# A fused attention and MLP kernel on one core: batch 0 in 24 single-exp slots, row sums of batch 1 moved out of the head, four MLP chunks begun early, and a weight matrix loaded by column halves

## The chip, the cores and the metric

The kernel runs on one core of a Trainium2 chip. The metric is the device time of one execution in microseconds (us), median of several; lower is better. The profile is of one execution of its own, and its span is about 2 us shorter than the device time. PE is TensorE (PEld its weight loads), DVE is VectorE, ACT is ScalarE, POOL is GpSimd, SP is SyncE, which issues the loads of q, k, v, U and V. The "granted clock" is the share of full TensorE clock that the throttle allowed.

## The reference, cut to what matters

```python
# q, k, v: 8 batches, 12 heads, 448 rows, 64 columns
q_n, k_n = rmsnorm(q, g_q), rmsnorm(k, g_k)
attn = softmax(q_n @ k_n.T / 8);  x = attn @ v            # per head; then heads side by side: 448 x 768
u  = x + (x.T @ U @ V).T                                  # U: 448 x 32, V: 32 x 448
out = u + relu(u @ w_ch1) @ w_ch2                         # w_ch1: 768 x 3072, w_ch2: 3072 x 768
```

## The kernel before

Heads are handled in pairs, six pairs to a batch; two pairs make a tile `t` (four heads of q, k and v). For each pair: squares and row sums, `rsqrt` (Ln and Exp on ACT), scaling, transposes on PE, scores in four blocks of keys, one exp of 112 x 896 per block, then values. The MLP of batch b runs as a generator `mlp(b)` whose pieces are woven between the pieces of `attention(b + 1)`. Batch 0's attention has no MLP to be woven with: this is the head. Score blocks have two PSUM buffers, called score banks below.

```python
def mlp(b):
    for hc in range(KH):                                   # 24 chunks: one "unit" of six matmuls each
        ph = ps_mm.tile([P, n], FP32, tag="mm")
        ...                                                # six matmuls, then relu: even on ACT, odd on DVE
        yield n
    for i in range(3 + par):                               # second product: row tile by row tile
        for half in range(2): ...                          # 24 matmuls each, four units; add u; store

def head():
    load(0, 2); load(1); load_v(0); load(2); load_mix(); ...      # load_mix loads U and V
    heat(NWARM)                                            # 16 warming matmuls, results unused
    ...
    rsqrt(1)
    setup_v()                                              # ACT casts V to bf16: waits for V's load
    scale(1, 0)
    ...
    for p in range(2, 7):                                  # one pair after another
        scores(p, (0, 1)); expo(p, 0); mix_a(0, p - 2); transposes(p + 1); expo(p, 1)
        ...
        values(p - 1, 0); heat(NH); scores(p, (2, 3)); expo(p, 2); values(p - 1, 1); mix_b(0, p - 2)
        expo(p, 3); scale(t + 1, odd); squares(t + 2, ALL, (odd,)); reduce(t + 2, ALL, (odd,))
        if p < 6: heat(NH)
        ...
# main: head(); load_w2 (row chunks) 0 to 2; then
rest = [(1, lambda i=i: mix_u(0, i)) for i in range(4)] + attention(1, 1)      # pairs 7 to 11
weave(fill, total * FA0, rest)
```

`squares` (POOL from tile 2 on) and `reduce` (DVE) make the row sums; `scale` is DVE, a `tensor_tensor` with both inputs in SBUF. `mix_u` adds the mixing term to x: PE, then two additions on DVE.

## Time and profile before

| | before |
|---|---|
| median of the first runs | 626.93 us (625.84 to 628.16) |
| span of the profile | 625.2 us |
| batch 0's MLP begins / batch 1's MLP begins | 56.0 us / 126.5 us |
| PE not busy, 11 to 57 us | 10.4 of 46 us |
| PE not busy, 57 to 126 us | 3.8 of 69 us |
| PE not busy, 126 to 205.8 us | 0.5 of 79.8 us |

The page of the profile has the span in 40 equal slices of 15.6 us; each digit is a busy share in tenths, and in the PEclk row the granted clock.

```profile
span 625.2 us, 11231 instructions
...
PE   5698999999999999999999999999999999999996
...
DVE  4688778146455466735546375935646365442211
ACT  5575662045430565145530465225441265302100
...
PEclk9599999999999999999999999999999999999999
DMA  9999988215535355655345356545155311040011
```

From the fifth slice on (62.5 us) every digit of PE up to the last slice is 9, so nearly all of the slack is at the front. The second clock digit is 5: in the second slice PE ran at about half its clock. The windows view gives busy time by stretch (the columns are the stretch, its length, the busy times of the engines with instruction counts, granted clock, DMA share and GB/s):

```profile
11.00:57.00 46.00, 35.59 (x397) 20.22 (x398) 35.10 (x85) 30.89 (x47) 25.56 (x23) 0.78 1.16 237
57.00:126.00 69.00, 65.16 (x577) 38.45 (x577) 44.23 (x97) 24.60 (x37) 16.68 (x13) 1.00 0.75 159
126.00:205.80 79.80, 79.27 (x605) 42.47 (x603) 40.85 (x91) 28.85 (x42) 14.32 (x9) 1.00 0.41 94
```

From 126 us on PE is the limit. The chain that ended last (start, us, what), up to 70 us, shows one thing that holds the head: V's load. ACT's next exps stand behind V's cast.

```profile
9.29 13.00 DMA Vf<-in_moe_V_dram
22.32 0.99 ACT V_90 L116
23.30 1.62 ACT E_96 L235 x2
```

The clock, again by the windows view, in stretches that follow the trace's clock record:

```profile
9.81:13.23 3.42, 1.16 (x12) 0.59 (x12) 2.40 (x7) 1.50 (x4) 0.00 (x0) 0.99 1.12 223
13.23:16.64 3.41, 1.76 (x14) 0.78 (x12) 2.76 (x5) 3.41 (x5) 0.25 (x1) 0.50 1.14 232
...
33.71:37.12 3.41, 3.00 (x44) 1.87 (x43) 2.62 (x6) 3.02 (x5) 0.23 (x1) 1.00 1.17 246
```

The clock stood at 0.50 for 20.5 us, until 33.7 us. In the kernel before, the throttled times read within the kernel are multiples of 3.41 us (20.5 us), so stretches of that length, cut where the clock changes, are called windows from here on.

### The profile page before, as it was taken

Reading aid. Unit: us, or ns where it says so; the run is one execution under the profiler, and the core shown is the slowest. Engines: PE = TensorE matmul, PEld = TensorE weight load, DVE = VectorE, ACT = ScalarE, POOL = GpSimd, SP = SyncE. Lnnn points to the kernel's source line nnn. Section 1 sums busy time; section 2 is a strip of 40 time slices with the busy share of each in tenths; the row PEclk is TensorE's granted clock in tenths of the full one; section 3 lists DMA queues with packets and bytes.
Section 4 is the critical chain, followed back from the end, with each engine's and each line's share of the span. In section 5 each row is a group of like instructions: output and inputs, shape, how many; then the busy total and the mean of one; then the engine's idle time right before and its main releaser. Section 6 shows DMA issues by size and latency. Waiting matters only on the chain.

```text
span 625.2 us, 11231 instructions
## 1 busy us (share of the span) xinstructions
PE 595.9 (95%) x4751; PEld 330.6 (53%) x4751; DVE 333.4 (53%) x735; ACT 235.6 (38%) x352; POOL 121.4 (19%) x101
## 2 busy tenths in 40 slices
PE   5698999999999999999999999999999999999996
PEld 2344555644555565544465555554556556554563
DVE  4688778146455466735546375935646365442211
ACT  5575662045430565145530465225441265302100
POOL 2656143011211121202221033303131020000000
PEclk9599999999999999999999999999999999999999
DMA  9999988215535355655345356545155311040011
GB/s 193 234 246 225 195 185 172 77 40 118 104 80 139 56 118 119 164 81 104 85 75 160 62 118 115 129 116 111 28 125 140 92 32 30 26 102 0 1 51 50
DMA packets 97913, 67.20 MB, mean 107 GB/s; under 512 B 54104, under 2 KB 94280, under 8 KB 97864
## 3 DMA queue, kind: packets, MB, share of 16 engines
q1 hardware_dynamic: 89732, 57.06, 40.3%
q0 software_dynamic: 7872, 9.44, 8.7%
q8 instruction: 37, 0.61, 0.4%
q14 instruction: 12, 0.10, 0.0%
q10 hardware_dynamic: 260, 0.00, 0.0%
HBM read 52.19 MB, written 11.01 MB: 101 GB/s over the span
## 4 chain that ended last, share of the span: by engine, by line
PE 79%; DVE 7%; DMA 6%; ACT 4%; issue 2%; POOL 1%; SPq 0%; POOLq 0%
PE po L351 33%; PE ph L336 30%; PE o L254 7%; PE sc L230 6%; DMA qkT<-qkn 2%; DMA Vf<-in_moe_V_dram 2%; DMA qk<-in_q_dram 2%; DVE qkn L201 1%; DVE osb L355 1%; DVE rstd L187 1%; ACT E_95 L235 1%; PE pu L293 1%; ACT hT L339 1%; ACT E_96 L235 1%; PE pt L214 1%
## 5 line engine op out<-in xcount | busy, mean ns | idle before, releaser
L351 PE MATMUL po<-w2b,hT 128*128 128x384 bf16 x1344 | 234.2, 326 | 2.9 <-DVE osb L355 2.9
L351 PEld LDWEIGHTS <-hT 128*128 128x128 bf16 x1344 | 126.8, 98 | 91.9 <-issue 13.5
L336 PEld LDWEIGHTS <-w1b 128*128 128x128 bf16 x1152 | 105.8, 98 | 105.6 <-issue 16.6
L339 ACT ACTIVATE hT<-ph 128x384 bf16<-128x384 f32 (+1 forms) x96 | 52.3, 545 | 253.0 <-PE ph L336 253.0
L181 POOL TENSOR_TENSOR sq<-qk 112x1024 f32<-112x1024 f32 x40 | 75.7, 1893 | 363.2 <-DVE rstd L187 232.2
L235 ACT ACTIVATE E_96<-sc 112x896 bf16<-112x896 f32 x96 | 85.9, 914 | 51.4 <-PE sc L230 51.4
L341 DVE TENSOR_SCALAR hT<-ph 128x384 bf16<-128x384 f32 (+1 forms) x96 | 59.6, 623 | 81.1 <-PE ph L336 80.3
L235 ACT ACTIVATE E_95<-sc 112x896 bf16<-112x896 f32 x96 | 85.8, 913 | 32.8 <-PE sc L230 32.7
L230 PE MATMUL sc<-qkT 64*112 64x448 bf16 x384 | 63.9, 386 | 9.7 <-ACT E_96 L235 4.4
L201 DVE TENSOR_TENSOR qkn<-qk,rstd 112x512 bf16<-112x512 f32 x88 | 59.6, 717 | 7.1 <-ACT rstd L193 7.0
L187 DVE TENSOR_REDUCE rstd<-sq 112x16 f32<-112x1024 f32 x44 | 53.2, 1209 | 2.4 <-POOL sq L181 2.0
L230 PEld LDWEIGHTS <-qkT 64*112 64x112 bf16 x384 | 22.0, 127 | 48.1 <-issue 43.3
L257 DVE RECIPROCAL rec<-o 128x4 f32<-128x4 f32 x96 | 17.1, 178 | 42.8 <-PE o L254 42.4
L254 PEld LDWEIGHTS <-E_95 112*128 112x128 bf16 x768 | 30.8, 99 | 9.8 <-issue 3.3
L254 PEld LDWEIGHTS <-E_96 112*128 112x128 bf16 x768 | 30.4, 99 | 7.6 <-issue 1.3
L336 PE MATMUL ph<-u_1555,w1b 128*128 128x512 bf16 x144 | 33.4, 379 | 0.0
L336 PE MATMUL ph<-u_3351,w1b 128*128 128x512 bf16 x144 | 33.3, 379 | 0.1
L336 PE MATMUL ph<-u_5057,w1b 128*128 128x512 bf16 x144 | 33.3, 379 | 0.0
L336 PE MATMUL ph<-u_6723,w1b 128*128 128x512 bf16 x144 | 31.2, 379 | 0.0
L336 PE MATMUL ph<-u_359,w1b 128*128 128x384 bf16 x144 | 27.1, 325 | 2.6 <-DVE hT L341 1.9
L336 PE MATMUL ph<-u_4220,w1b 128*128 128x384 bf16 x144 | 25.8, 326 | 0.1
L336 PE MATMUL ph<-u_5926,w1b 128*128 128x384 bf16 x144 | 25.8, 326 | 0.0
(111 smaller groups left out, 402.2 us busy)
## 6 DMA issues: line engine op xcount, KB each, us to landing
vt<-in_v_dram SPq DMA_DIRECT2D x22, 448.0 KB, 6.8
qk<-in_q_dram SPq DMA_DIRECT2D x21, 448.0 KB, 4.5
qk<-in_k_dram SPq DMA_DIRECT2D x21, 448.0 KB, 6.0
w1b<-in_moe_w_ch_dram POOLq DMA_DIRECT2D x6, 768.0 KB, 18.3
w2b<-in_moe_w_ch_dram POOLq DMA_DIRECT2D x6, 768.0 KB, 10.2
out_dram<-osb SPq DMA_DIRECT2D x8, 336.0 KB, 2.8
out_dram<-osb SPq DMA_DIRECT2D x8, 288.0 KB, 2.6
out_dram<-osb SPq DMA_DIRECT2D x8, 240.0 KB, 2.6
```

The source lines that it names most:

```text
L181: nc.gpsimd.tensor_tensor(sqs[t, s][:, hs], qks[t][:, s, hs], qks[t][:, s, hs], OP.mult)
L187: nc.vector.tensor_reduce(rstds[t][:, s, hs].rearrange("p h j -> p (h j)"), sqs[t, s][:, hs].rearrange("p h (j d) -> p (h j) d", d=D), AX, ...
L201: nc.vector.tensor_tensor(qkns[t][:, pr, s].rearrange("p j h d -> p h j d"), qk[:, s, hp].rearrange("p h (j d) -> p h j d", d=D), rstd[:, ...
L214: nc.tensor.transpose(pt.rearrange("d s (j p) -> d (s j) p", j=NJ)[:, i, :], qkn[:, i, :], ident[:SP, :SP])
L230: nc.tensor.matmul(sc[:, hh, 0:S], kT[pp, kc * SP:(kc + 1) * SP], qT[pp, :], start=True, stop=True)
L235: nc.scalar.activation(Es[p % NE][:, :, PAD + kc * S:PAD + (kc + 1) * S], scs.pop((p, kc))[:, :, 0:S], AF.Exp, scale=float(D) ** 0.5)
L254: nc.tensor.matmul(o[:, i, :], E[:, hh, c:c + P], va[:, hl, kc, :], start=(kc == 0), stop=(kc == NJ - 1))
L257: nc.vector.reciprocal(rec, o[:, :, D])
L336: nc.tensor.matmul(ph, w1b[:, dc, hc * P:(hc + 1) * P], u[:, dc, :], start=(dc == 0), stop=(dc == KD - 1))
L339: nc.scalar.activation(hT[:, hc, 0:n], ph, AF.Relu)
L341: nc.vector.tensor_relu(hT[:, hc, 0:n], ph)
L351: nc.tensor.matmul(po, hT[:, hc, i * P:(i + 1) * P], w2b[:, hc, hs], start=(hc == 0), stop=(hc == KH - 1))
```

## The change

Its intent: run the head at ACT's pace, one exp per slot, with everything else fitted between; let values lag by two pairs; take V's cast off ACT's critical place; take tiles 3's and 4's row sums out of the head; use the score banks, free after the last exp, to begin the MLP; issue w2 later and by column halves, because its area now also holds squares.

```diff
-    early = w2b[:, 0:11, :]...                    # squares of tiles 0 and 1
+    early = w2b[:, 0:22, :]...                    # squares of tiles 0 to 3
-    NE, NV, NWARM, NH = 2, 3, 16, 3
-    FA, FM, NPE, FA0 = 0.77, 0.09, 14, 0.5
+    NE, NV, NWARM, NH = 3, 3, 16, 2
+    FA, FM, NPE, FA0 = 0.77, 0.09, 14, 0.66
...
-    def load_w2(i):           # four rows of 128
+    def load_w2(half, i):     # eight rows of 128, one half of the columns
...
+        order = [(i, h) for h in range(2) for i in range(n)] if b == 0 else [(i, h) for i in range(n) for h in range(2)]
...
 # attention(b), within a pair p of tile t:
+            if t + 1 < NT and not odd:
+                add(0, reduce, t + 1, ALL, (1,))
             add(1, expo, p, 1)
...
+            if t + 1 < NT and odd:
+                add(0, scale, t + 1, 1)
+                add(0, cast_v, t + 1)             # POOL cast, now right behind the scale
...
 # head:
+        at(1, squares, 1, ALL, (1,));  at(1, reduce, 1);  at(1, yield_port, 0, 1);  at(1, squares, 2)
+        at(2, heat, NH);  at(3, rsqrt, 1);  at(3, scale, 1, 0);  ...;  at(4, heat, NH)
+        at(5, transposes, 2);  ...;  at(10, values, 0, 0);  at(11, values, 0, 1);  at(11, setup_v)
+        ...;  at(21, values, 4, 0);  at(22, values, 4, 1);  ...
+        for n in range(24):
+            expo(*divmod(n, 4))
+            for piece in fill[n]: piece()
+            if n + 2 < 24: scores((n + 2) // 4, ((n + 2) % 4,))
+        first(0, range(0, 3), True)               # MLP chunks 0 to 3, in two score tiles
+        values(5, 0);  values(5, 1);  mix_b(0, 4);  first(0, (3,), False);  first(1, range(0, 4), True)
+        ...;  mix_b(0, 5);  reduce(3);  rsqrt(3)
+        first(0, (5,), False);  first(1, (5,), False)
+        scale(3, 0);  scale(3, 1);  squares(4, ALL, (0,))
...
+        late = {6 + i: [(load_w2, *divmod(i, 3))] + ([(mix_u, 0, i - 1)] if 0 < i < 5 else []) for i in range(6)}
+                rest = [(4, lambda: (transposes(6), reduce(4, ALL, (0,)), squares(4, ALL, (1,))))] + attention(1, late)
```

`yield_port` is a tiny POOL copy that reads a scaled tile, so that POOL's next work starts after DVE's scale. Each entry of `late` runs at the end of its pair. The diff holds more that the cut leaves out: four of six copies of `mix_b` went from ACT to DVE, relus 1, 3 and 5 of batch 0 from DVE to ACT, V's load went ahead of the first load of v, and w1 comes in four loads instead of six.

More of the change, by code (lines that the diff above doesn't have):

```diff
@@ L76 @@
     spare = hT.rearrange("p k n -> p (k n)").bitcast(FP32).rearrange("p (t s h e) -> p t s h e", t=2, s=3, h=HG)
-    early = w2b[:, 0:11, :].rearrange("p k n -> p (k n)")[:, 0:8192].bitcast(FP32).rearrange("p (t s h e) -> p t s h e", t=2, s=2, h=HG)
+    early = w2b[:, 0:22, :].rearrange("p k n -> p (k n)")[:, 0:16384].bitcast(FP32).rearrange("p (t s h e) -> p t s h e", t=4, s=2, h=HG)
     Ub = consts.tile([P, 2, 4, rank], BF16, name="Ub")
@@ L136, in load_w1 @@
     def load_w1(i):
-        c = slice(512 * i, 512 * (i + 1))
+        c = (slice(0, 512), slice(512, 1024), slice(1024, 2048), slice(2048, 3072))[i]
         nc.gpsimd.dma_start(w1b[:, :, c], w1r[:, :, c])
-    def load_w2(i):
-        c = slice(4 * i, 4 * (i + 1))
-        nc.gpsimd.dma_start(w2b[:, c, :], w2r[:, c, :])
+    def load_w2(half, i):
+        c, d = slice(8 * i, 8 * (i + 1)), slice(half * HALF, (half + 1) * HALF)
+        nc.gpsimd.dma_start(w2b[:, c, d], w2r[:, c, d])
     NT, NP = B * 3, B * 6
@@ L175, in squares @@
             if (t, s) not in sqs:
-                sqs[t, s] = early[0:SP, t, s] if t < 2 else norm.tile([SP, HG, NJ * D], FP32, tag="sq", name="sq", bufs=1)
+                sqs[t, s] = early[0:SP, t, s] if t < 4 else norm.tile([SP, HG, NJ * D], FP32, tag="sq", name="sq", bufs=1)
             if t < 2:
@@ L321, in mix_b @@
             nc.tensor.matmul(pu[:, i * P:(i + 1) * P], xt[i][:, cs], ident, start=False, stop=(i == 2))
-        nc.scalar.activation(us[b][:, dc, :], pu, AF.Copy)
+        if dc in (0, 5):
+            nc.scalar.activation(us[b][:, dc, :], pu, AF.Copy)
+        else:
+            nc.vector.tensor_copy(us[b][:, dc, :], pu)
     def store(b, c0, c1, osb, r0):
@@ L332, in mlp @@
         u, n = us[b], (384, 512)[par]
-        for hc in range(KH):
+        for hc in range(0 if b else 4, KH):
             ph = ps_mm.tile([P, n], FP32, tag="mm")
@@ L337, in mlp @@
                                  start=(dc == 0), stop=(dc == KD - 1))
-            if hc % 2 == 0:
+            if hc % 2 == 0 or (b == 0 and hc < 7):
                 nc.scalar.activation(hT[:, hc, 0:n], ph, AF.Relu)
@@ L342, in mlp, with attention @@
             yield n
-        xt = x_tiles(b)
-        for i in range(3 + par):
+        xt, n = x_tiles(b), 3 + par
+        order = [(i, h) for h in range(2) for i in range(n)] if b == 0 else [(i, h) for i in range(n) for h in range(2)]
+        osbs = {}
+        for i, half in order:
             off = OFFS[par][i]
-            osb = opool.tile([P, dm], FP32, tag="osb")
-            for half in range(2):
-                hs = slice(half * HALF, (half + 1) * HALF)
-                po = ps_mm.tile([P, HALF], FP32, tag="mm")
-                for hc in range(KH):
-                    nc.tensor.matmul(po, hT[:, hc, i * P:(i + 1) * P], w2b[:, hc, hs],
-                                     start=(hc == 0), stop=(hc == KH - 1))
-                    if hc % 6 == 5 and hc != KH - 1:
-                        yield HALF
-                nc.vector.tensor_add(osb[:, hs], po, xt[i][:, hs])
-                if half == 1:
-                    if off < 0:
-                        store(b - 1, 384, 448, osb, 0)
-                        store(b, 0, 64, osb, 64)
-                    else:
-                        store(b, off, off + P, osb, 0)
-                yield HALF
-    def attention(b, start=0):
+            if half == 0:
+                osbs[i] = opool.tile([P, dm], FP32, tag="osb", name="osb")
+            hs = slice(half * HALF, (half + 1) * HALF)
+            po = ps_mm.tile([P, HALF], FP32, tag="mm")
+            for hc in range(KH):
+                nc.tensor.matmul(po, hT[:, hc, i * P:(i + 1) * P], w2b[:, hc, hs],
+                                 start=(hc == 0), stop=(hc == KH - 1))
+                if hc % 6 == 5 and hc != KH - 1:
+                    yield HALF
+            nc.vector.tensor_add(osbs[i][:, hs], po, xt[i][:, hs])
+            if half == 1:
+                osb = osbs.pop(i)
+                if off < 0:
+                    store(b - 1, 384, 448, osb, 0)
+                    store(b, 0, 64, osb, 64)
+                else:
+                    store(b, off, off + P, osb, 0)
+            yield HALF
+    def attention(b, extra={}):
         items = []
@@ L369, in add @@
             items.append((weight, lambda: fn(*args)))
-        for p in range(b * 6 + start, b * 6 + 6):
+        for p in range(b * 6, b * 6 + 6):
             t, odd = divmod(p, 2)
-            add(1, scores, p, (0, 1))
+            add(2 if p == 6 else 1, scores, p, (0, 1))
             add(0, expo, p, 0)
@@ L376, in attention @@
                 add(1, transposes, p + 1)
+            if t + 1 < NT and not odd:
+                add(0, reduce, t + 1, ALL, (1,))
             add(1, expo, p, 1)
-            if not odd and t + 1 < NT:
-                add(0, rsqrt, t + 1)
             if p % 6:
                 add(1, values, p - 1, 0)
+            if t + 1 < NT and not odd:
+                add(0, rsqrt, t + 1)
             if p + 1 < NP:
                 add(0, gains, p + 1)
-            if t + 1 < NT:
-                add(0, scale, t + 1, odd)
+            if t + 1 < NT and odd:
+                add(0, scale, t + 1, 1)
+                add(0, cast_v, t + 1)
             add(1, scores, p, (2, 3))
@@ L389, in attention @@
                 add(1, values, p - 1, 1)
-            if t + 2 < NT:
-                add(0, squares, t + 2, ALL, (odd,))
-            if t + 1 < NT and odd:
-                add(0, cast_v, t + 1)
             add(1, expo, p, 3)
-            if t + 2 < NT and p != 8:
-                add(0, reduce, t + 2, ALL, (0, 1) if p == 9 else (odd,))
-            if odd and t + 3 < NT:
+            if t + 1 < NT and not odd:
+                add(0, scale, t + 1, 0)
+                add(0, squares, t + 2, ALL, (0,)) if t + 2 < NT else None
+            if t + 2 < NT and odd:
+                add(0, reduce, t + 2, ALL, (0,))
+                add(0, squares, t + 2, ALL, (1,))
+            for fn, *args in extra.get(p, ()):
+                add(0, fn, *args)
+            if odd and 6 <= t + 3 < NT:
                 add(0, load, t + 3)
                 add(0, load_v, t + 3)
-            if 8 <= p <= 10:
-                add(0, load_w2, p - 5)
         add(1, values, b * 6 + 5, 0)
@@ L410, in head @@
         load(1)
-        load_v(0)
         load(2)
         load_mix()
+        load_v(0)
         load_v(1)
@@ L429, in head @@
         reduce(0, Bh, (1,))
+        squares(1, ALL, (0,))
         rsqrt(0, Bh)
         scores(0, (0, 1))
-        expo(0, 0)
-        scale(0, 1)
-        transposes(1)
-        expo(0, 1)
-        squares(1)
-        squares(2, ALL, (0,))
-        cast_v(0)
-        load_w1(0)
-        load_w1(1)
-        nc.gpsimd.tensor_copy(Uc, Uf)
-        scores(0, (2, 3))
-        expo(0, 2)
-        scores(1, (0, 1))
-        expo(0, 3)
-        reduce(1)
-        rsqrt(1)
-        setup_v()
-        scale(1, 0)
@@ L450, in head @@
-        reduce(2, ALL, (0,))
-        load(4)
-        load_v(4)
-        heat(NH)
-        expo(1, 0)
-        values(0, 0)
-        expo(1, 1)
-        scores(1, (2, 3))
-        expo(1, 2)
-        setup_u(0)
-        values(0, 1)
-        transposes(2)
-        expo(1, 3)
-        squares(2, ALL, (1,))
-        cast_v(1)
-        load_w1(2)
-        setup_u(1)
-        scale(1, 1)
-        reduce(2, ALL, (1,))
-        load(5)
-        load_v(5)
-        for p in range(2, 7):
-            t, odd = divmod(p, 2)
-            scores(p, (0, 1))
-            expo(p, 0)
-            mix_a(0, p - 2)
-            transposes(p + 1)
-            expo(p, 1)
-            if not odd:
-                rsqrt(t + 1)
-            values(p - 1, 0)
-            if p == 6:
-                values(5, 1)
-                mix_b(0, 4)
-                mix_a(0, 5)
-            else:
-                heat(NH)
-            scores(p, (2, 3))
-            expo(p, 2)
-            if p == 6:
-                mix_b(0, 5)
-            else:
-                values(p - 1, 1)
-                mix_b(0, p - 2)
-            expo(p, 3)
-            scale(t + 1, odd)
-            squares(t + 2, ALL, (odd,))
-            reduce(t + 2, ALL, (odd,))
-            if p < 6:
-                heat(NH)
-            if odd:
-                cast_v(t + 1)
-            if p < 5:
-                load_w1(p + 1)
@@ new lines, in head, with at @@
+        fill = {n: [] for n in range(24)}
+        def at(n, fn, *args):
+            fill[n].append(lambda: fn(*args))
+        at(0, scale, 0, 1)
+        at(0, transposes, 1)
+        at(1, squares, 1, ALL, (1,))
+        at(1, reduce, 1)
+        at(1, yield_port, 0, 1)
+        at(1, squares, 2)
+        at(1, load_w1, 0)
+        at(2, heat, NH)
+        at(3, rsqrt, 1)
+        at(3, scale, 1, 0)
+        at(3, yield_port, 1, 0)
+        at(3, nc.gpsimd.tensor_copy, Uc, Uf)
+        at(3, cast_v, 0)
@@ new lines, in head @@
+        at(3, heat, NH)
+        at(4, heat, NH)
+        at(5, transposes, 2)
+        at(5, scale, 1, 1)
+        at(5, yield_port, 1, 1)
+        at(5, cast_v, 1)
+        at(5, load_w1, 1)
+        at(6, setup_u, 0)
+        at(6, heat, 1)
+        at(7, heat, NH)
+        at(7, reduce, 2, ALL, (0,))
+        at(8, transposes, 3)
+        at(8, reduce, 2, ALL, (1,))
+        at(8, cast_v, 2)
+        at(9, setup_u, 1)
+        at(9, heat, 1)
+        at(10, values, 0, 0)
+        at(11, values, 0, 1)
@@ new lines, in head @@
+        at(11, setup_v)
+        at(11, rsqrt, 2)
+        at(11, scale, 2, 0)
+        at(12, mix_a, 0, 0)
+        at(12, heat, 1)
+        at(13, transposes, 4)
+        at(13, scale, 2, 1)
+        at(13, load, 4)
+        at(13, load_v, 4)
+        at(13, load_w1, 2)
+        at(14, values, 1, 0)
+        at(14, yield_port, 2, 1)
+        at(14, squares, 3)
+        at(15, values, 1, 1)
+        at(16, transposes, 5)
+        at(16, load, 5)
+        at(16, load_v, 5)
+        at(16, load_w1, 3)
@@ new lines, in head @@
+        at(16, cast_v, 3)
+        at(16, mix_b, 0, 0)
+        at(17, values, 2, 0)
+        at(18, values, 2, 1)
+        at(18, mix_a, 0, 1)
+        at(19, values, 3, 0)
+        at(19, mix_b, 0, 1)
+        at(20, values, 3, 1)
+        at(20, mix_a, 0, 2)
+        at(21, values, 4, 0)
+        at(21, mix_b, 0, 2)
+        at(22, values, 4, 1)
+        at(22, mix_a, 0, 3)
+        at(23, mix_b, 0, 3)
+        at(23, mix_a, 0, 4)
+        for n in range(24):
+            expo(*divmod(n, 4))
+            for piece in fill[n]:
+                piece()
+            if n + 2 < 24:
+                scores((n + 2) // 4, ((n + 2) % 4,))
@@ new lines, in head @@
+        first(0, range(0, 3), True)
+        values(5, 0)
+        values(5, 1)
+        mix_b(0, 4)
+        first(0, (3,), False)
+        first(1, range(0, 4), True)
+        mix_a(0, 5)
+        first(0, (4,), False)
+        first(1, (4,), False)
+        mix_b(0, 5)
+        reduce(3)
+        rsqrt(3)
+        first(0, (5,), False)
+        first(1, (5,), False)
+        scale(3, 0)
+        scale(3, 1)
+        squares(4, ALL, (0,))
+    scratch = consts.tile([1, 1], BF16, name="scratch")
@@ new lines, in yield_port, with first @@
+    def yield_port(t, pr):
+        nc.gpsimd.tensor_copy(scratch, qkns[t][0:1, pr, 1, 0, 0, 0:1])
+    firsts = {}
+    def first(i, dcs, start):
+        if start:
+            firsts[i] = ps_s.tile([P, 2, 512], FP32, tag="s", name="first")
+        ph, u = firsts[i], us[0]
+        for hh in range(2):
+            hc = 2 * i + hh
+            for dc in dcs:
+                nc.tensor.matmul(ph[:, hh, 0:384], w1b[:, dc, hc * P:(hc + 1) * P], u[:, dc, :],
+                                 start=(dc == 0), stop=(dc == KD - 1))
+        if dcs[-1] == KD - 1:
+            nc.scalar.activation(hT[:, 2 * i:2 * i + 2, 0:384], ph[:, :, 0:384], AF.Relu)
@@ L527, in heat, with volume @@
                 nc.tensor.matmul(warm, xss[1][:, 0:P], xss[1][:, 0:512], start=True, stop=True)
-    def volume(par):
-        n = (384, 512)[par]
-        return 24 * n + (6 + 2 * par) * 4 * HALF
+    def volume(b):
+        n = (384, 512)[b % 2]
+        return (24 if b else 20) * n + (6 + 2 * (b % 2)) * 4 * HALF
     with tc.manual_schedule():
         head()
-        for i in range(3):
-            load_w2(i)
+        late = {6 + i: [(load_w2, *divmod(i, 3))] + ([(mix_u, 0, i - 1)] if 0 < i < 5 else []) for i in range(6)}
         for b in range(B):
-            fill, total = mlp(b), volume(b % 2)
+            fill, total = mlp(b), volume(b)
             if b + 1 < B:
-                rest = [(1, lambda i=i: mix_u(0, i)) for i in range(4)] + attention(1, 1)
+                rest = [(4, lambda: (transposes(6), reduce(4, ALL, (0,)), squares(4, ALL, (1,))))] + attention(1, late)
                 weave(fill, total * (FA if b else FA0), attention(b + 1) if b else rest)
```

## The prediction

> **What bounds the kernel now.** Span 625.2 us. By the windows view TensorE (PE) is busy 79.3 of 79.8 us in batch 1's MLP stage and 63.7 of 64.6 us in the next: from 126 us on, PE work is the limit, at full granted clock, and the change leaves that work alone. What can move is the start of batch 1's MLP, now at 126 us, plus up to 2 us of stalls later.
>
> **The head.** The first exp starts at 12.2 us, batch 0's MLP at 56 us. From 11 to 57 us ACT is busy 30.9 and DVE 35.1 of 46 us. The chain of waits: the V load (13.0 us) blocks ACT's queue until 22.3 us; from 36 us on each pair goes round PE, exp and DVE in 5.07 us, of which 1.3 us are warming matmuls. The granted clock is 0.50 from 14 to 33 us. [...]
>
> **What the change does.** Twenty-four exps x 0.865 = 20.8 us; with squares, rsqrt, V cast and mix copies about 26 us on ACT. V no longer blocks ACT; values two pairs late don't wait for exp. DVE becomes the limit: scales 5 x 1.29, evictions of transposes 5 x 0.83, reductions 5.5, twelve values x 0.74, mixing copies 3.5, U 0.7: about 29 us from 11 us on, so 40 without gaps[...]. ([...] a scale took 1517 ns beside a POOL cast, median 686.) Reduce(3), rsqrt and scale, about 4.5 us, are covered on PE by the four early chunks (3.9 us) and three more. So near 49 us PE has seven of 48 MLP units (0.97 us each) and six pairs done. Left: 41 x 0.97 = 40, values 6, scores 6, transposes 3.5, mixing 5: about 61 us, and 4 to 5 of stalls, as in this stage before (PE idle 3.8 of 69). Batch 1's MLP starts at about 114 us instead of 126. The later order of reduce and scale may give or take 1 us.
>
> **What may eat it.** DMA runs at 235-247 GB/s up to 56 us; about 24 MB land before 126 us now, and by 114 us that is 210 GB/s. w2's column halves are released only as pairs 6 to 11 end; the last is issued about 6 us before its use, against a median landing of 10.2 us.
>
> **Predicted:** 613.8 us, range 605 to 622. Faster by over 2%: 0.54; within 2%: 0.43; slower: 0.03.
>
> **Signs.** Right: the 24 exps at about 1.15 us spacing, the last at 38-42 us; clock 1.00 before 28 us; DVE over 85% busy from 13 to 42 us; first relu of batch 0 near 45-48 us; batch 1's MLP starts at 112-116 us; later stages within 1 us. Wrong: slots stretch over 1.3 us, waiting for loads or POOL; PE waits over 2 us for w1 or w2 between 46 and 105 us; later stages grow.
>
> **What would make it wrong.** Upwards: DMA saturation delaying tile 4 or w2's last part, DVE held by POOL. Downwards: earlier clock release and DVE without gaps, giving 607.

Three passages are cut from it. Two state how the hardware behaves where no trace of this case shows it. The third is a term of the sum: to the 40 us of DVE's work without gaps the author added an allowance of 3 to 4 us, an estimate, so that this sum came to 43 to 44 us; the 49 us, the 114 us and the 613.8 us that follow were reached with it.

## The result, and the profile after

The changed kernel took 618.49 us (617.73 to 619.76, four runs) against 626.91 us (four runs). Ratios here are the mean time of one kernel's fast runs over that of the other's of the same rounds, so not quite the ratio of the medians: 0.9867, interval 0.9841 to 0.9893. It is faster by 1.3%, inside the 2% band, and inside the predicted range.

```profile
span 618.0 us, 11193 instructions
...
PE   5888799999999999999999999999999999999996
...
DVE  4976887264643775656555566745646365442211
ACT  5946552055410664055430555135531365202100
...
PEclk9899999999999999999999999999999999999999
```

The second clock digit went from 5 to 8. V's load is gone from the chain. The windows view, for the slots, the stage of batch 0's MLP once seven of its 48 units are done, and the stage of batch 1's MLP:

```profile
12.00:42.00 30.00, 25.40 (x337) 15.23 (x340) 24.08 (x66) 24.11 (x33) 16.94 (x19) 0.94 1.15 232
...
49.60:119.00 69.40, 61.35 (x569) 36.29 (x567) 49.51 (x102) 26.51 (x40) 21.73 (x16) 1.00 0.95 186
119.00:198.40 79.40, 78.35 (x596) 42.21 (x601) 42.58 (x91) 28.85 (x42) 14.76 (x9) 1.00 0.42 95
```

The last exp of the head ends at 38.8 us, and at 49.6 us seven units of the MLP are done, as predicted. Batch 1's MLP begins at 118.95 us instead of 126.54, 7.6 us earlier; from there to the end it is 499.0 us against 498.7 before. So the whole gain is made before 119 us.

But in the middle line PE has no work for 69.40 - 61.35 = 8.05 us; the same stage before idled 3.8 us. The PE timeline shows where. The bracket at the end of a line is the idle time just before it and what ended it.

```profile
56.79 0.40 PE L230 MATMUL sc<-qkT 64*112 64x448 bf16 x2 [1.07 <-ACT E_95 L235]
57.98 0.40 PE L230 MATMUL sc<-qkT 64*112 64x448 bf16 x2 [0.79 <-ACT E_95 L235]
...
65.48 0.32 PE L293 MATMUL pu<-t4b,V_90 128*128 128x384 bf16 x1 [0.90 <-DVE hT L344]
68.04 0.55 PE L214 MATMUL pt<-ident,qkn 112*128 112x112 bf16 x8 [0.75 <-DVE x_340 L294]
...
76.58 1.14 PE L339 MATMUL ph<-u_399,w1b 128*128 128x384 bf16 x6 [1.52 <-DVE x_340 L294]
...
109.86 9.26 PE L357 MATMUL po<-w2b,hT 128*128 128x384 bf16 x56 [0.46 <-DMA w2b<-in_moe_w_ch_dram]
```

There are three main kinds: scores waiting for exps at 57 us (1.86 us), PE waiting for DVE's relus and `mix_u` additions (line 294), and w2's last part (0.46 us only). ACT's timeline tells why the exps were late: `rsqrt` of tile 4 stands in ACT's queue before two exps of pair 6 and waits for DVE's row sum, one of those that the change moved here.

```profile
53.22 0.91 ACT L235 ACTIVATE E_95<-sc 112x896 bf16<-112x896 f32 x1
55.35 0.32 ACT L192 ACTIVATE rstd<-rstd,eps 112x32 f32<-112x32 f32 x1 [1.22 <-DVE rstd L187]
55.70 0.23 ACT L193 ACTIVATE rstd<-rstd 112x32 f32<-112x32 f32 x1
55.84 0.90 ACT L235 ACTIVATE E_95<-sc 112x896 bf16<-112x896 f32 x1
```

### The profile page after: what moved, and what is told of

Same layout as the page of the kernel before. It is cut to its first block, busy times and chain, and to the rows that moved or that the text cites. A ratio compares the mean times of both kernels' runs of the same rounds, so it can differ in the third digit from the quotient of the medians.

```text
span 618.0 us, 11193 instructions
## 1 busy us (share of the span) xinstructions
PE 588.1 (95%) x4712; PEld 328.1 (53%) x4735; DVE 343.0 (56%) x736; ACT 235.0 (38%) x349; POOL 123.3 (20%) x105
## 4 chain that ended last, share of the span: by engine, by line
PE 83%; DVE 6%; ACT 4%; DMA 4%; issue 1%; POOL 1%; POOLq 0%; DVEq 0%
PE po L357 32%; PE ph L339 32%; PE o L254 7%; PE sc L230 7%; DMA qkT<-qkn 3%; DVE rstd L187 2%; ACT E_95 L235 1%; DVE osb L361 1%; DMA w2b<-in_moe_w_ch_dram 1%; PE warm L579 1%; DVE qkn L201 1%; ACT hT L342 1%; PE pt L214 1%; PE pu L293 1%; PE first L552 1%
## 5 line engine op out<-in xcount | busy, mean ns | idle before, releaser
L339 PEld LDWEIGHTS <-w1b 128*128 128x128 bf16 x1128 | 103.8, 98 | 103.4 <-issue 15.1
L344 DVE TENSOR_SCALAR hT<-ph 128x512 bf16<-128x512 f32 (+1 forms) x93 | 58.1, 624 | 79.7 <-PE ph L339 78.9
L235 ACT ACTIVATE E_97<-sc 112x896 bf16<-112x896 f32 x64 | 56.9, 913 | 44.2 <-PE sc L230 44.2
L201 DVE TENSOR_TENSOR qkn<-qk,rstd 112x512 bf16<-112x512 f32 x88 | 64.9, 777 | 1.7 <-ACT rstd L193 1.5
L235 ACT ACTIVATE E_96<-sc 112x896 bf16<-112x896 f32 x64 | 56.7, 914 | 19.7 <-PE sc L230 19.1
L187 DVE TENSOR_REDUCE rstd<-sq 112x16 f32<-112x1024 f32 x40 | 48.5, 1213 | 11.9 <-POOL sq L181 11.6
L339 PE MATMUL ph<-u_3330,w1b 128*128 128x512 bf16 x138 | 32.6, 379 | 0.4 <-issue 0.2
L339 PE MATMUL ph<-u_5036,w1b 128*128 128x512 bf16 x138 | 32.6, 379 | 0.4 <-issue 0.2
L339 PE MATMUL ph<-u_1595,w1b 128*128 128x512 bf16 x138 | 32.6, 379 | 0.4 <-issue 0.2
L339 PE MATMUL ph<-u_6703,w1b 128*128 128x512 bf16 x141 | 31.1, 379 | 0.2
L339 PE MATMUL ph<-u_5905,w1b 128*128 128x384 bf16 x144 | 25.8, 326 | 0.0
L339 PE MATMUL ph<-u_2493,w1b 128*128 128x384 bf16 x144 | 25.6, 326 | 0.0
L339 PE MATMUL ph<-u_4199,w1b 128*128 128x384 bf16 x144 | 25.6, 326 | 0.0
L339 PE MATMUL ph<-u_399,w1b 128*128 128x384 bf16 x120 | 22.5, 326 | 1.5 <-DVE x_340 L294 1.5
```

Of the source, the lines that this page charges most:

```text
L187: nc.vector.tensor_reduce(rstds[t][:, s, hs].rearrange("p h j -> p (h j)"), sqs[t, s][:, hs].rearrange("p h (j d) -> p (h j) d", d=D), AX, ...
L201: nc.vector.tensor_tensor(qkns[t][:, pr, s].rearrange("p j h d -> p h j d"), qk[:, s, hp].rearrange("p h (j d) -> p h j d", d=D), rstd[:, ...
L235: nc.scalar.activation(Es[p % NE][:, :, PAD + kc * S:PAD + (kc + 1) * S], scs.pop((p, kc))[:, :, 0:S], AF.Exp, scale=float(D) ** 0.5)
L339: nc.tensor.matmul(ph, w1b[:, dc, hc * P:(hc + 1) * P], u[:, dc, :], start=(dc == 0), stop=(dc == KD - 1))
L344: nc.vector.tensor_relu(hT[:, hc, 0:n], ph)
```

## The experiments

Twelve kernels ran, each five rounds against the kernel before. Where a small difference matters, read the clock column with the time: the mean granted clock of an execution turned out to vary by itself. "Batch 1" is where its MLP begins in the profiled execution. Kernels e1 to e4, e5 to e8, e9 to e11, and e12 each shared a chip and the runs of the kernel before.

| run | median us (range) | mean clock of the runs | ratio to before | batch 1, us |
|---|---|---|---|---|
| before | 626.4 to 627.3 | 0.982 to 0.988 | 1 | 126.5 |
| changed, first result | 618.49 (617.73 to 619.76) | 0.993 to 0.996 | 0.9867 | 118.95 |
| e1 changed again | 619.12 (617.99 to 623.79) | 0.978 to 0.997 | 0.9905 | 117.5 |
| e2 before, V cast late | 623.64 (622.35 to 625.59) | 0.987 to 0.991 | 0.9959 | 122.6 |
| e3 no warming in the slots | 621.46 (620.96 to 622.33) | 0.979 to 0.984 | 0.9922 | 122.05 |
| e4 no early chunks | 619.79 (617.67 to 623.17) | 0.979 to 1.000 | 0.9898 | 123.8 (clock low) |
| e5 tile 4's sums, own buffers | 620.26 (617.61 to 623.34) | 0.979 to 0.998 | 0.9907 | 123.1 (clock low) |
| e6 mix_u first | 621.48 (620.83 to 623.87) | 0.987 to 0.996 | 0.9926 | 121.8 |
| e7 POOL cast after scale | 618.22 (616.50 to 625.32) | 0.978 to 0.996 | 0.9879 | 120.4 |
| e8 tile 3's sums earlier | 619.36 (618.19 to 622.83) | 0.982 to 0.997 | 0.9892 | 119.7 |
| e9 warming over the gaps | 618.53 (616.99 to 619.34) | 0.995 to 0.999 | 0.9859 | 118.6 |
| e10 w2 by rows, issued early | 623.54 (622.69 to 625.29) | 0.983 to 0.994 | 0.9946 | 122.3 |
| e11 combined | 616.98 (615.50 to 618.07) | 0.996 to 0.999 | 0.984 | 116.1 |
| e12 combined, DVE relieved | 616.06 (615.42 to 616.40) | 0.995 to 1.000 | 0.9831 | 114.8 |

### e1: the changed kernel again

> The changed kernel unaltered, as the reference for the runs on this chip. Expected 618 to 619 us and 0.986 to 0.988 of the kernel before.

The median, 619.12 us, is within 0.7 us of the first result (the ratio, 0.9905, is above what was expected), but the five runs spread over 5.8 us and go with the clock: 617.99 us at 0.997, 620.28 at 0.989, 623.79 at 0.978. The kernel before has no such spread in clock. One kernel, two speeds: this had to be explained before anything else could be read, and e5's profiled execution, which has the same slots as the changed kernel, happened to catch the slow case. First the changed kernel, by the windows view in steps of the clock record:

```profile
12.28:15.70 3.42, 1.79 (x14) 0.84 (x15) 2.84 (x5) 3.42 (x6) 1.49 (x2) 1.00 1.14 223
15.70:19.11 3.41, 2.98 (x9) 0.76 (x9) 2.76 (x4) 2.73 (x6) 3.24 (x3) 0.50 1.13 215
19.11:22.52 3.41, 3.41 (x33) 1.65 (x31) 2.94 (x7) 3.37 (x5) 0.61 (x3) 1.00 1.12 211
```

Then e5:

```profile
11.88:15.30 3.42, 1.80 (x14) 0.84 (x15) 2.58 (x5) 3.39 (x6) 0.67 (x2) 1.00 1.14 222
15.30:18.71 3.41, 2.72 (x9) 0.63 (x9) 2.76 (x3) 2.72 (x6) 3.41 (x3) 0.50 1.13 213
...
35.78:39.19 3.41, 2.96 (x54) 2.22 (x52) 1.79 (x7) 2.80 (x5) 3.41 (x4) 1.00 1.13 239
```

In both, a window in which PE was busy for about half the time (1.79 and 1.80 us) is followed by a throttled one. In the first the next window is 2.98 us busy and the clock returns; in the second it is 2.72 us busy, and the clock stays at 0.50 for 20.5 us. Both throttled windows hold the same three warming matmuls (1.64 and 1.65 us), but measured from these matmuls the window lies about 0.26 us later in the first and takes in that much more of the other work. What decides between the two is not shown. PE's busy share alone does not: in e5 PE was busy for the whole of the next three windows (18.71 to 28.95 us), and the clock stayed at 0.50. That it was really low there is seen by the matmuls: a pair for the scores took 0.62 us at 18.67 us and 0.40 us at 62.13 us. Batch 0's first ordinary MLP chunk begins at 46.4 us in e1's profile and at 52.3 us in e5's. For later comparison, this is e1's stage from there to batch 1's MLP:

```profile
46.38:117.49 71.11, 64.22 (x585) 37.99 (x584) 50.52 (x106) 29.04 (x45) 21.74 (x16) 1.00 0.95 188
```

PE has no work for 6.9 us of it. The same stretch of the first profile, from 46.7 to 118.95 us, has 8.05 us. So two executions of one kernel differ by over 1 us in this stage, with the clock at 1.00 in both.

### e2: the kernel before, with V's cast moved

```diff
         rsqrt(1)
-        setup_v()
         scale(1, 0)
...
         cast_v(1)
         load_w1(2)
+        setup_v()
```

> The kernel before, with only the cast of V to bf16 moved from ahead of pair 1's exps to behind them, so that ACT's queue no longer waits for V's load. Theory (the slots: six pairs at 5.07 us each set the head, the V wait is a part of it): batch 0's MLP begins 3 to 4 us earlier and the total falls by 2 to 4 us. Rival (the V wait is most of the head's loss): the total falls by 6 us or more, most of the change's 8.4 us. If neither: within 1 us of the kernel before, because loads set the pace.

The total fell by 2.8 us (626.43 to 623.64), as the slots theory said, and batch 0's MLP began at 51.75 instead of 56.0 us. The rival falls: V's wait was not most of the loss. Not all of the 2.8 us is the wait itself, for the throttled time in the profile also fell, from 20.5 to 10.2 us, in two stretches.

### e3: no warming matmuls in the slots

```diff
-        at(2, heat, NH)
...                                  # and the other six heat entries
```

> The changed kernel without the eleven warming matmuls in the slots (the sixteen at the start stay). Theory A (warming is what brings the clock back at 19 us instead of 33 us): granted clock stays 0.50 to beyond 24 us and the total rises by 1.5 to 4 us. Theory B (the denser slots alone keep TensorE busy enough): clock back within 2 us of the same instant, total within 1 us, perhaps lower.

Theory A holds: the clock stayed at 0.50 from 13.5 to 34.0 us in the profile, all six runs have 0.979 to 0.984, and the median is 621.46 us, 2.3 us above e1. The spread is only 1.4 us. This also splits the change's gain. The new schedule with a late clock is worth 5.0 us (626.43 to 621.46). Against that, e1's best run, with the clock back at once, is 3.5 us faster (617.99 us), and its worst, at a mean clock of 0.978, 2.3 us slower (623.79 us); that warming matmuls at half clock crowd the slots would explain the second (in the changed kernel's profile one took 0.61 us at 17.84 us, at a clock of 0.50, and 0.39 us at 20.49 us, at 1.00), but was not tested. So warming here is a bet.

### e4: no early MLP chunks

```diff
-        for hc in range(0 if b else 4, KH):
+        for hc in range(KH):
...                                  # and the seven first(...) calls removed
```

> The changed kernel without the four MLP chunks begun in the score banks; they run in the ordinary loop. Theory (they fill TensorE while DVE sums, ACT takes rsqrt and DVE scales tile 3): batch 0's first ordinary chunks start at about the same time and the total rises by 3 to 4 us. Rival (DVE's queue sets the next pairs' start anyway, so the fill is worth little): rises by less than 1.5 us.

The rival holds. The median rose by 0.7 us, which the spread of the clock covers; its best run (617.67 us) is as good as e1's best. In two executions with a late clock, e4 begins batch 1's MLP at 123.8 us and e5, which has the early chunks, at 123.1 us. Without them the ordinary loop simply begins 2.9 us earlier (49.4 against 52.3 us), so four chunks of 0.97 us win about 1 us there and 0.7 us at batch 1 (and e4's clock came back one window later, at 38.9 against 35.8 us, so even that is generous).

### e5: separate buffers for tile 4's squares

```diff
-                sqs[t, s] = early[0:SP, t, s] if t < 4 else norm.tile(...)
+                sqs[t, s] = early[0:SP, t % 4, s] if t < 5 else norm.tile(...)
```

> The changed kernel; the squares of tile 4 go to two places of w2's area instead of one shared buffer, so POOL's second half no longer waits for DVE's sum of the first. Theory H1 (this chain DVE sum, POOL square, DVE sum, rsqrt on ACT, exps makes TensorE idle for 2.9 us between 54 and 58 us): the idle falls below 1 us and the total by 1.5 to 3 us. Rival (DVE's backlog would hold TensorE a little later all the same): total within 0.7 us.

H1 falls. POOL's second square did start earlier relative to the stage, but PE still idled 0.81 and 0.79 us before the two scores, and the best run (617.61 us) is that of the changed kernel. The wait that mattered is ACT's, for the row sum on DVE, which in e5 stands behind other DVE work (in the changed kernel it waited 0.17 us more for POOL's square).

### e6: mix_u at the start of the stage

```diff
-  ... + ([(mix_u, 0, i - 1)] if 0 < i < 5 else []) for i in range(6)}
-  rest = [(4, ...)] + attention(1, late)
+  ... for i in range(6)}
+  rest = [(1, lambda i=i: mix_u(0, i)) for i in range(4)] + [(4, ...)] + attention(1, late)
```

> The changed kernel with batch 0's four mix_u pieces back at the start of the stage, as in the kernel before, instead of one at the end of each of pairs 7 to 10. Theory H2 (spread out, each piece stands behind DVE's queue and TensorE waits for it, some 4.5 us in four places): total falls by 1 to 3 us. Rival (at the start they collide with tile 3's and 4's sums and scales): total rises by 1 to 2 us.

H2 falls, the rival holds: at clocks of 0.995 and 0.996 the four runs took 620.83 to 622.95 us, where the changed kernel's three in the first result took 617.73 to 619.76 us. Spreading `mix_u`, which the change did without its title saying so, is worth some 2 to 3 us, in spite of the waits that one sees at each piece.

### e7: POOL's cast behind the scale

```diff
                 add(0, scale, t + 1, 1)
+                add(0, yield_port, t + 1, 1)
                 add(0, cast_v, t + 1)
```

> The changed kernel with one tiny POOL copy ahead of the V cast in each odd pair that reads the scaled tile, so POOL's cast starts only after DVE's scale. Theory H3 (the scales took 2.62, 1.81 and 2.12 us for two instead of 1.29 [...], and TensorE's waits for mix_u follow them): scales in the stage go back to 1.3 us for two, the total falls by 1 to 2.5 us. Rival: POOL starts its later squares and w2 issues later, total within 0.7 us or up.

The effect on the scales is shown. In the changed kernel, DVE's timeline has two scales in 2.62 us, while POOL squares until 61.75 us and casts from 62.63 us, and later two in 2.12 us, while POOL casts from 90.63 to 91.68 us:

```profile
62.22 2.62 DVE L201 TENSOR_TENSOR qkn<-qk,rstd 112x512 bf16<-112x512 f32 x2
...
90.72 2.12 DVE L201 TENSOR_TENSOR qkn<-qk,rstd 112x512 bf16<-112x512 f32 x2
```

In e7:

```profile
64.11 1.29 DVE L201 TENSOR_TENSOR qkn<-qk,rstd 112x512 bf16<-112x512 f32 x2
...
90.77 1.28 DVE L201 TENSOR_TENSOR qkn<-qk,rstd 112x512 bf16<-112x512 f32 x2
```

Beside POOL's work the scales took 1.3 us longer in one place and 0.8 us in the other; by what mechanism is not shown. But the first place is not the edit's doing alone: without the edit the same two scales took 1.29 us in e10's profile, where POOL's cast ended at 62.32 us, 0.13 us after they began, and 1.29 us in e5's, where they began at 67.56 us and the cast had ended at 62.98 us. There the cast lay beside the two scales before them, which took 2.84 us. The second place took 2.12 us in the changed kernel's profile and 1.28 us in e7's. The tiny copy itself took 0.18 us. The value is less clear: the best runs are 616.50 and 616.63 us against 617.73 and 617.89, but one run was 625.32 us at a clock of 0.978. Taken alone, the gain is inconclusive.

### e8: tile 3's row sums earlier

```diff
         first(0, range(0, 3), True)
+        reduce(3)
         values(5, 0)
...
         mix_b(0, 5)
-        reduce(3)
         rsqrt(3)
```

> The changed kernel with DVE's two row sums of tile 3 (2.33 us) moved up ahead of the evictions of pair 5, into gaps where DVE idles 2.5 us between 39 and 44.5 us. Theory (the sums that the change moved out of the head load DVE's queue when the next stage starts): DVE is 1.5 to 2.3 us ahead at 50 us, the total falls by 1 to 2 us. Rival (it delays the evictions that mixing's last two columns wait for, so the MLP starts later): total rises by 0.5 to 2 us.

Neither: 618.19 to 622.83 us, as e1, and the waits of 1.07 and 0.79 us at 57 us are unchanged. Its profile shows what can follow those waits:

```profile
55.39:58.80 3.41, 1.55 (x10) 0.68 (x8) 1.90 (x4) 3.20 (x6) 0.12 (x1) 1.00 0.67 179
58.80:62.21 3.41, 3.41 (x19) 2.00 (x17) 1.30 (x3) 0.15 (x1) 3.41 (x3) 0.51 0.14 38
```

PE was busy for only 1.55 us of one window, and the next one ran at half clock, in the middle of the MLP. It happened at the same place in e7's and e9's profiles (in e7's a second time, at 109.8 us), but not in those of the changed kernel, e1 or e11.

### e9: warming matmuls over the gaps

```diff
         transposes(0)
+        heat(3)
...
         scores(0, (0, 1))
+        heat(5)
...
+        at(1, heat, NH)
```

> The changed kernel with ten more warming matmuls, put into gaps in which TensorE waits anyway: three behind the first transposes, five behind the first scores, two in slot 1. Theory (the clock is throttled at 14 to 16 us because the 3.41 us window before it held only 0.33 to 0.53 of TensorE work, and whether it comes back at 18 or at 36 us is chance, worth 5 us): the window before 15.5 us fills to over 0.75, the mean granted clock is above 0.990 in every run, the slow runs of 622 to 624 us vanish and the median falls to 616 to 618 us. Rival (the added matmuls hold up the transposes and scores): the clock is high but the median stays at 619 us or rises.

What the theory said of the clock came true. In all four runs the mean clock is 0.995 to 0.999, and no run was above 619.34 us. The stretches that e9 changed are these:

```profile
10.00:13.40 3.40, 2.84 (x18) 0.94 (x16) 2.63 (x5) 2.83 (x5) 0.04 (x1) 1.00 1.12 248
13.40:16.80 3.40, 3.25 (x18) 1.13 (x20) 3.00 (x4) 2.74 (x4) 3.40 (x3) 1.00 1.14 238
```

The clock was 1.00 from 6.6 to 57.8 us. How PE's activity sets the clock is not shown beyond this. The median, 618.53 us, is not below that of the lucky runs and misses the 616 to 618 us expected. A likely reason, not tested, is that in those only one window of 3.41 us was throttled, at a time when PE had slack; and e9's own profile has a throttled window at 57.8 us. What the edit buys is that the slow case did not occur. The ten runs of e11 and e12, which contain the edit, bear it out: all 14 have a mean clock of at least 0.995, against 14 of the 39 runs of the first result, e1 and e4 to e8, which have the changed kernel's slots and warming.

### e10: w2 by rows, issued early

```diff
-   c, d = slice(8 * i, 8 * (i + 1)), slice(half * HALF, (half + 1) * HALF)
+   c = slice(4 * i, 4 * (i + 1))                  # all columns; row tiles in the old order
...
-   late = {6 + i: [(load_w2, *divmod(i, 3))] ...
+   late = {6 + i: ([(load_w2, 2 * i), (load_w2, 2 * i + 1)] if i < 3 else []) ...
```

> The changed kernel with w2 loaded in six row chunks, as in the kernel before, and batch 0's second product in the old order, but with two chunks issued at the end of each of pairs 6, 7 and 8 instead of one at each of 6 to 11. Theory (the column halves only allow a later issue; w2's area is free from 47 us on, so an earlier issue does the same): total within 0.3% of the changed kernel at like clock. Rival (row chunks make the first product wait): TensorE idles over 2 us for w2 near 83 us and the total rises by 2 us or more.

The theory falls: 623.54 us, and 622.79 us even at a clock of 0.994, some 4 us worse. PE waited 1.34 us for w2 at 92.5 us, less than the rival said. The rest came by another way. DVE's timeline:

```profile
72.78 3.18 DVE L201 TENSOR_TENSOR qkn<-qk,rstd 112x512 bf16<-112x512 f32 x2
75.99 1.02 DVE L294 TENSOR_TENSOR x<-pu,x 128x384 bf16<-128x384 f32 x2
```

Two scales took 3.18 us beside POOL's square, two w2 issues and a cast; PE then waited 2.89 us for the additions at 76 us, and was throttled from 77.4 to 80.8 us. So the run shows that rows issued early are worse; it doesn't separate the row chunks from the early issue. e11 issued early too, by column halves, and waited for w2 nowhere. That suggests that column halves help, but e11 has other edits as well, so it isn't shown, and by how much stays open.

### e11: a combination

```diff
+   # the ten warming matmuls of e9, the yield_port of e7
-            if t + 1 < NT and not odd:
+            if t + 1 < NT and not odd and p != 6:
                 add(0, rsqrt, t + 1)
...                                               # behind the last exp of the pair:
+            if p == 6:
+                add(0, rsqrt, t + 1)
...
-   late = {6 + i: [(load_w2, *divmod(i, 3))] ...
+   late = {6 + i: ([(load_w2, *divmod(2 * i, 3)), (load_w2, *divmod(2 * i + 1, 3))] if i < 3 else []) ...
```

> The changed kernel with four edits together: the ten warming matmuls of e9, rsqrt of tile 4 behind the last exp of pair 6 (ACT waited 1.2 us for it at 54 us and TensorE 1.9 us for the exps), the POOL cast after the scale (e7), and w2's column halves issued two per pair at pairs 6 to 8. Expected: idle before scores at 57 us below 0.8 us, none for w2, batch 1's MLP near 114 us, clock above 0.990 in every run, median 613 to 616 us, which is faster than both kernels. Rival (a stall removed comes back as the next one on DVE): median 616.5 us or above in spite of the clock.

616.98 us, and the clock was 0.996 to 0.999 in every run. One of the two waits for exps is gone (0.79 us), the other is still 1.06 us. None is left for w2. But the wait for `mix_u`'s addition that was 1.52 us in the changed kernel's profile (1.36 in e1's and e9's) grew to 1.86 us, at 74.7 us, behind scales that took 2.15 us (1.29 us in e12's profile, where POOL's square was held back until they had ended). So part of the rival came true. The stage from the first ordinary MLP chunk:

```profile
46.34:116.10 69.76, 64.16 (x587) 37.94 (x584) 50.50 (x106) 29.12 (x45) 22.01 (x19) 1.00 0.95 192
```

PE has no work for 5.6 us of it, against 6.9 in e1. The median missed the 613 to 616 us expected. It is 1.5 us below that of e9, which has the same warming, but the ranges of the two overlap.

### e12: the combination, with DVE relieved

```diff
-            if hc % 2 == 0 or (b == 0 and hc < 7):
+            if hc % 2 == 0 or (b == 0 and (hc < 7 or hc % 4 != 3)):
...
+                    add(0, yield_port, t + 1, 0)
                     add(0, squares, t + 2, ALL, (0,))
```

> The kernel of e11 with two more edits that relieve DVE in the stage of batch 0's MLP: four of its nine relus there go to ACT (ACT is busy 29 of 70 us), and POOL's square after a scale of the even pair starts only when that scale has ended, by a tiny POOL copy (in e11 that scale took 2.15 us for two against 1.29, and TensorE then waited 1.86 us for mix_u). Theory (DVE's queue is what holds TensorE in this stage): the waits of TensorE for DVE's additions between 60 and 95 us fall from 2.8 us to below 1 us, batch 1's MLP starts 1.5 to 2.5 us earlier at 113.6 to 114.6 us, median 614.5 to 615.5 us. Rival (ACT's exps now stand in front of the relus and TensorE waits for score banks instead, or the batch's last values do): batch 1's MLP within 0.7 us of e11, median within 1 us of 617 us.

The PE timeline:

```profile
56.99 0.40 PE L230 MATMUL sc<-qkT 64*112 64x448 bf16 x2 [1.06 <-ACT E L235]
...
73.87 1.14 PE L339 MATMUL ph<-u,w1b 128*128 128x384 bf16 x6 [1.00 <-DVE x L294]
...
82.34 0.55 PE L214 MATMUL pt<-ident,qkn 112*128 112x112 bf16 x8 [0.44 <-DVE x L294]
```

and the stage from its first ordinary MLP chunk to batch 1's MLP, by the windows view:

```profile
46.60:114.80 68.20, 64.03 (x586) 37.81 (x585) 47.21 (x102) 30.63 (x49) 22.47 (x22) 1.00 0.97 195
```

The waits for additions between 60 and 95 us fell to 1.44 us, not quite below 1 us; PE lacks work for 4.2 us of the stage, and batch 1's MLP begins at 114.8 us. Batch 1's MLP moved by 1.3 us, less than the theory said (1.5 to 2.5) and more than the rival did (0.7). The median is 616.06 us, 0.9 us below e11: above the theory's range, and just inside the rival's "within 1 us of 617". The intervals of e11 and e12 overlap, so this last step is not clear of noise by time, only by the trace. All five runs lie within 1 us, and all are faster than each of e9's four (616.99 to 619.34 us, on another chip), which have the same warming. It has the lowest median, 1.7% below the kernel before (ratio 0.9831, interval 0.9815 to 0.9846).

## Why the prediction was right or wrong, point by point

- **What bounds it.** Right. From batch 1's MLP on nothing changed (499.0 against 498.7 us), and the gain was the earlier start of that MLP.
- **The head.** Right in its sum. The exps end at 38.8 us (said: 38 to 42), 1.1 us apart (said: 1.15), the first relu is at 47.5 us (said: 45 to 48), seven units are done at 49.6 us (said: 49). Its reason was off: it had DVE as the limit, with about 29 us of work without gaps. DVE was busy 24.1 of the 30 us from 12 to 42 us, 80% and not over 85%, and ACT just as long, so the slots had no single limit, and that the exps ended where they were said to is in part luck.
- **The step that failed** is a term of the sum: "4 to 5 of stalls, as in this stage before". The work was right (said 61, PE was busy 61.35 us), the stalls were 8.05 us in the profiled execution and 6.9 us in e1's. Batch 1's MLP began at 119 us (117.5 in e1) and not 114. Of these 5 us the stalls are 3 to 4; the start at 49.6 instead of 49 us and 0.35 us of work are about 1. Together they are about the difference between 613.8 and 618.5 us. The stage was not the one of before. DVE was busy 49.5 of 69.4 us in it, against 44.2 of 69.0 before: its queue had got the row sums of tiles 3 and 4 that the head had lost, its scales took longer beside POOL's work (2.62, 1.81 and 2.12 us for two instead of 1.29), and `rsqrt` of tile 4 stood in front of exps. What e11 and e12 show: edits aimed at these waits, on top of e9's warming, bring the idle time from 8.05 or 6.9 us (two profiles of the changed kernel) to 5.6 and 4.2 us, and batch 1's MLP to 116.1 and 114.8 us. With the stalls at 4.2 us, within what was forecast, it begins within 1 us of the forecast 114. How the stalls divide among the causes is not shown: single edits (e5, e7, e8) did not show a gain clear of the spread, and e8 speaks against tile 3's sums as a large part.
- **What may eat it.** DMA was named first and was not it: PE waited 0.46 us for w2's last part (0.57 to 1.01 us in the profiles of e1 and e3 and e5 to e9) and never for w1. "DVE held by POOL" was named too, and came true: two scales took 2.62 us and 2.12 us beside POOL's casts, and 1.29 and 1.28 us in e7's profile.
- **The clock.** "1.00 before 28 us" came true in the profiled execution (19.1 us). It is not a property of the kernel: mean clock and time vary from run to run, and of the 39 runs of kernels with these slots (first result, e1, e4 to e8) six had a mean of 0.983 or less, and these took 622.8 us or more. None of the first four was among them, which is partly luck. The prediction gave no weight to the late case. In e5 the clock stayed at 0.50 through three windows in which PE was busy throughout.
- **The verdict.** "Faster by over 2%" was given 0.54, and it came out within 2% (0.43); the range of 605 to 622 us held.

Left open: how much column halves alone are worth; what the changes named below the diff, never run alone, are worth; why the clock stayed at 0.50 through those three windows of e5; what besides PE's busy share goes before a fall of the clock (in e2 a window with PE busy for 2.20 us, 22.15 to 25.57 us, was followed by one at 0.50, in the changed kernel one with 2.11 us, 8.87 to 12.28 us, was not); and what the last 1.06 us of PE's wait at 57 us would be worth.

## What to carry to other kernels

Work that is moved out of a stage lands in the queue of some engine in the next one (here DVE's, busy for 49.5 of 69.4 us after the change and 44.2 of 69.0 before): count that engine's queue, not only its busy share, before booking the gain. When a kernel's times spread, list them beside the granted clock of each execution first; with warming in the slots alone the mean clock of the 39 runs was anywhere from 0.978 to 1.000, and with warming put into gaps in which TensorE waits anyway the mean clock was 0.995 or more in all 14 runs of e9, e11 and e12. Where DVE's scales take longer while POOL squares or casts (here 2.12 us for two, against 1.28), make POOL wait by a tiny dependent copy (0.18 us), but judge it in combination, as the stall it removes may be followed by the next.
